# Cells of an mLSTM kernel moved to four ticks for every three units, and the first product of two groups taken as three float32r products

## The chip, the cores and the metric

One NeuronCore of a Trainium2 chip runs the whole kernel. The metric is the device time of the kernel in microseconds. Three runs of the kernel before are shown; their median counts.

## What is computed

An mLSTM cell over 4 batches, 8 heads, 768 steps and 40 channels, and behind it a feed-forward layer on its output, 3072 tokens of 320 channels through 2048 hidden ones. The reference, cut to what matters:

```python
for t in range(S):
    m_new = np.maximum(f_gate[:, :, t] + m, i_gate[:, :, t])
    f_stab = np.exp(f_gate[:, :, t] + m - m_new)
    i_stab = np.exp(i_gate[:, :, t] - m_new)
    C = f_stab * C + i_stab * np.einsum('bhd,bhe->bhde', vt, kt)
    n = f_stab * n + i_stab * kt
    y[:, :, t] = o * np.einsum('bhde,bhe->bhd', C, qt) / np.maximum(np.abs(n . qt), 1.0)
x = y.transpose(0, 2, 1, 3).reshape(B * S, H * D)
h = x @ w_in
out = np.maximum(0.01 * h, h) @ w_out
```

## The kernel before

**Chunks and groups.** The 768 steps are cut into NB = 6 chunks of 128. Cell s = 4c + b is chunk c of batch b, all 8 heads: 24 cells. Group g is the feed-forward layer on the 512 tokens (4 batches x 128 steps) of chunk g. Chunk 0 is worked out ahead of everything. After that the loop at the end of the kernel runs six passes, c = 1 to 6: pass c issues the layer of group c - 1 unit by unit, and in the gaps the cells of chunk c. So the cells of chunks 2 to 5 lie beside groups 1 to 4, and group 5 has none.

**A group's units.** `ff_units` makes 16 units of first product (a pair j of 128-column blocks of w_in, each pair in two units: 5 slots of 64 rows x 2 row halves, L759, then Prelu on ScalarE, L767) and for groups 1 to 5 the 14 units of `fast_units`, a Strassen-like second product in 7 products of two row blocks n, in the order p1, p2, p6, p7, p4, p5, p3 (L835). Sums lie on VectorE and GpSimd: p1 makes s1 and s2 (L853, L858), p2 empties its bank at L862, p6 makes s4 (L870) and adds on GpSimd (L868), p7 adds at L876, p4 at L882, both on GpSimd, p5 empties its bank at L887 into both halves of y on VectorE, p3 at L892. The banks of ph and po come from one pool of four (`psf`, tag mm), the cells' from another of four (`psc`).

**A cell.** `u_parts` multiplies k, q and the state's parts (L614, L619) and puts them with the mask weights w into `qn` (L624, VectorE). `u_mix` takes the tanh of o (ScalarE), multiplies (L695, pT), turns and scales the result on VectorE and GpSimd (L702, L706, L709, L713), carries the state on (L592 on GpSimd, L596 on VectorE) and stores x to DRAM (L716). `ahead(s)` prepares a cell: `prep_kq` turns k and q into kqT (L505, L511, VectorE), the loads of k, q and ea for cell s + 2 are issued (L398, L421), and the state and k are scaled on GpSimd. `feed(s)` loads k, v and w (L356, L359, L413). `prep_mask` adds the mask to w on GpSimd (L450). `gather_x` loads a cell's x back as xT, whose one buffer serves group after group (L730).

**What sets the order.** Instructions of TensorE, VectorE, ScalarE and GpSimd run in the order in which the code issues them (`manual_schedule`). Only SyncE's queue, through which nearly all transfers go, is ordered by the framework. Per group of 30 units i the table below places the cells' nine units (two u_parts, two u_mix, two u_parts, the gates, two u_mix) and the masks; o and the feed follow a u_mix, `ahead` follows it too, but not between i = 16 and 23.

```python
masks = {0: (2, 3), 12: (4, 5)}
pairs = (2, 2, 6, 6, 14, 14, 19, 19, 19)
```

Of the kernel before, what the change touches and what calls it, by code (L numbers as in the profile page):

```python
# [10 lines left out]
U32 = mybir.dt.uint32  # L11
U64 = mybir.dt.uint64
# [6 lines left out]
def kernel(  # L19
# [58 lines left out]
    dr = ctx.enter_context(tc.tile_pool(name="dr", bufs=1, space=bass.MemoryType.DRAM))  # L78

# [39 lines left out]
    kn = consts.tile([P, NL, H, DP], F32, name="kn")  # L119
    qn = consts.tile([P, NL, H, DP], F32, name="qn")  # L120
    S_t = [consts.tile([P, 2, H, DP], F32, name=f"S{n}") for n in range(NL)]
    S_v = [t[:].rearrange("p u h (k d) -> p u h k d", d=QW) for t in S_t]
    rb_t = [consts.tile([P, 3, RW], F32, name=f"rb{n}") for n in range(NR)]
    xb = consts.tile([P, PR * TB, QW], F32, name="xb")
# [147 lines left out]
    def gates(c):  # L272
# [5 lines left out]
        F = wk.tile([n, P], F32, name="F", bufs=1)  # L278
        nc.vector.tensor_tensor_scan(F[:], fc, zeros[:n].to_broadcast([n, P]), 0.0, op0=ALU.add, op1=ALU.add)
        if c > 0:  # L280
            il_t = wk.tile([BH, P], F32, name="il", bufs=1)
            nc.vector.tensor_scalar(il_t[:], il, scalar1=m0[:], scalar2=None, op0=ALU.subtract)
            il = il_t[:]
        m = wk.tile([n, P], F32, name="m", bufs=1)
        nc.vector.tensor_tensor_scan(m[:], fc, il, -1e30 if c == 0 else 0.0, op0=ALU.add, op1=ALU.max)
        a = wk.tile([n, P], F32, name="a", bufs=1)
        nc.vector.tensor_tensor(a[:], F[:], m[:], op=ALU.subtract)
        bu = wk.tile([BH, 3, P], F32, name="bu", bufs=1)
# [117 lines left out]
    def spread(s):  # L406
# [3 lines left out]
        w = wk.tile([P, H, P], F32, name="w", bufs=NL)  # L410
# [4 lines left out]
    def spread_q(s):  # L415
# [3 lines left out]
        d["ea"] = wk.tile([P, H, SL], F32, name="ea", bufs=EAB)  # L419
# [5 lines left out]
    def spread_first(a, s2):  # L425
# [12 lines left out]
        for n in range(2):  # L438
            w = st[s2 + n]["w"] = wk.tile([P, H, P], F32, name="w", bufs=NL)
# [20 lines left out]
    def prep_vu(s):  # L460
# [3 lines left out]
        if s < NS:  # L464
            d["vu"] = wk.tile([P, H, 2, V1], F32, name="vu")
# [34 lines left out]
    def prep_kq(s):  # L500

        d = st[s]
        d["kqT"] = wk.tile([P, 2, PR * P], F32, name="kqT")
# [20 lines left out]
    def u_split(s):  # L524

        d = st[s]
        d["kqT"] = wk.tile([P, 2, PR * P], F32, name="kqT")
# [14 lines left out]
    def u_transpose(s):  # L542
        d = st[s]
        d["kqT"] = wk.tile([P, 2, PR * P], F32, name="kqT")
# [92 lines left out]
    def u_values(s):  # L637
# [4 lines left out]
        d["den"] = wk.tile([P, H], F32, name="den")  # L642
        denominators(d["den"][:], pa[:, :, D])

    def gate(s):

        d = st[s]
        d["x"] = wk.tile([P, Dm], F32, name="x")
# [7 lines left out]
    def u_plain(s):  # L656
# [13 lines left out]
        den = wk.tile([P, H], F32, name="den")  # L670
        denominators(den[:], hN[:, :, 0, DB])
        if b < 2:
            d["x"] = wk.tile([P, Dm], F32, name="x")[:]
# [10 lines left out]
    def u_mix(s):  # L684
# [16 lines left out]
        hb = wk.tile([P, PR * TB, QW], F32, name="hb", bufs=1)  # L701
        nc.vector.transpose(hb[:].rearrange("p (j n) d -> p j n d", n=TB), in_blocks(pT[:]))  # L702
        den = wk.tile([P, PR * TB], F32, name="den")
# [8 lines left out]
        xq = wk.tile([P, PR * P], F32, name="x")  # L712
# [6 lines left out]
    def gather_x(s):  # L719

        c, b = divmod(s, B)
        if ("xT", c) not in st:
            st["xT", c] = wk.tile([P, KC, GT], F32, name="xT", bufs=1)
        xT = st["xT", c]
# [410 lines left out]
```

## Time and profile before

| What | us |
|---|---|
| three runs | 514.08, 512.78, 509.91 |
| their median | 512.78 |
| span of the profiled execution (no time beside it is given) | 508.0 |
| TensorE busy in it | 492.0 |
| VectorE busy | 308.1 |
| ScalarE busy | 171.5 |
| GpSimd busy | 137.7 |

Lines such as L759 are lines of the kernel before. PE is TensorE's matmuls, PEld its weight loads, DVE VectorE, ACT ScalarE, POOL GpSimd, SP SyncE. A name with q behind it (SPq) is that engine's own instruction queue, which issues transfers and waits. A busy TensorE is not one at its peak, since matmuls overlap.

### The profile page before, as it was taken

How to read it: one execution, taken by the hardware profiler on the slowest of the kernel's cores; microseconds unless marked ns; L12 is line 12 of the kernel's file. 1: busy time of each engine (PE TensorE's matmuls, PEld its weight loads, DVE VectorE, ACT ScalarE, POOL GpSimd, SP SyncE). 2: the span in 40 equal slices, each digit the busy share in tenths (PEclk: the TensorE clock that was granted, in tenths of full speed). 3: DMA queues.
4: the chain of work that ended last, by engine and by line, in shares of the span. 5: the costliest groups of instructions: out<-in, count | busy, mean ns of one | idle time of the engine just before them, and what ended most of it. 6: DMA issues, size and time to landing. Idle time of an engine off the chain costs nothing.

```text
span 508.0 us, 12526 instructions
## 1 busy us (share of the span) xinstructions
PE 492.0 (97%) x4981; PEld 366.6 (72%) x4981; DVE 308.1 (61%) x515; ACT 171.5 (34%) x478; POOL 137.7 (27%) x175
## 2 busy tenths in 40 slices
PE   8878999999999999999999999999899999999997
PEld 7766878767655489955589855599755599744797
DVE  4779898899954778635765826764825664101321
ACT  3664864652722510323411323311213411022210
POOL 4243443360402404413104614014612003000020
PEclk9877999999999999999999999999999999999999
DMA  9977687888765551565663566564466212200001
GB/s 116 146 204 154 149 219 185 168 152 175 155 145 87 131 124 46 133 130 144 147 132 92 115 137 170 137 141 97 109 135 177 68 53 62 69 1 1 1 1 52
DMA packets 165290, 59.21 MB, mean 117 GB/s; under 512 B 128816, under 2 KB 156016, under 8 KB 165232
## 3 DMA queue, kind: packets, MB, share of 16 engines
q1 hardware_dynamic: 164848, 58.28, 52.2%
q8 instruction: 39, 0.64, 0.5%
q14 instruction: 19, 0.16, 0.1%
q10 hardware_dynamic: 384, 0.13, 0.1%
HBM read 51.68 MB, written 6.70 MB: 115 GB/s over the span
## 4 chain that ended last, share of the span: by engine, by line
PE 79%; DVE 9%; DMA 3%; ACT 3%; POOL 2%; issue 2%; SPq 2%; ACTq 0%; POOLq 0%; DVEq 0%
PE ph L759 36%; PE po L835 26%; PE po L794 6%; PE pT L695 3%; PE sd L614 3%; SPq L359 1%; PE sd L619 1%; DMA S<-in_v_dram 1%; ACT kqT L540 1%; PE tkq L548 1%; DVE raw L261 1%; DMA rb<-in_q_dram 1%; DMA w<-a_dr 1%; PE pa L641 1%; DVE qn L511 1%
## 5 line engine op out<-in xcount | busy, mean ns | idle before, releaser
L759 PE MATMUL ph<-xT,w_in 64*128 64x512 f32 (+1 forms) x1120 | 216.2, 538 | 2.4 <-DVE y L887 1.4
L759 PEld LDWEIGHTS ph<-xT,w_in 64*128 64x128 f32 x1120 | 108.6, 189 | 95.1 <-issue 86.3
L767 ACT ACTIVATE acts<-ph 128x512 f32<-128x512 f32 (+1 forms) x112 | 53.9, 533 | 179.0 <-PE ph L759 178.9
L835 PEld LDWEIGHTS po<-w_out,acts 128*128 128x128 f32 x640 | 87.3, 190 | 3.8 <-issue 3.8
L835 PE MATMUL po<-w_out,acts 128*128 128x160 f32 x640 | 89.1, 300 | 0.0
L450 POOL TENSOR_TENSOR w<-w,i 128x512 f32<-128x512 f32 x20 | 26.9, 1345 | 117.3 <-DMA w<-a_dr 117.2
L624 DVE TENSOR_TENSOR qn<-w,sd 64x512 f32<-64x512 f32 x40 | 27.4, 684 | 40.2 <-PE sd L619 20.5
L458 ACT ACTIVATE w<-w,gT 128x64 f32<-128x64 f32 (+1 forms) x192 | 50.8, 348 | 2.7 <-POOL w L450 1.7
L592 POOL TENSOR_TENSOR S<-S,f 40x336 f32<-40x336 f32 x36 | 32.0, 889 | 67.3 <-PE pT L695 36.3
L835 PE MATMUL po<-raw,acts 128*128 128x160 f32 x320 | 45.5, 300 | 0.0
L835 PEld LDWEIGHTS po<-raw,acts 128*128 128x128 f32 x320 | 43.9, 190 | 0.3
L794 PE MATMUL po<-w_out,acts 128*128 128x320 f32 x128 | 36.5, 436 | 0.0
L702 DVE STREAM_TRANSPOSE hb<-pT 128x512 f32<-128x512 f32 x16 | 11.5, 717 | 31.0 <-PE pT L695 30.8
L794 PEld LDWEIGHTS po<-w_out,acts 128*128 128x128 f32 x128 | 23.6, 190 | 9.3 <-issue 0.3
L511 DVE TENSOR_TENSOR qn<-kqT,ea 64x512 f32<-64x512 f32 x32 | 28.4, 888 | 1.0
L709 POOL TENSOR_TENSOR xb<-xb,den 128x320 f32<-128x320 f32 x16 | 11.7, 729 | 56.8 <-DVE xb L706 56.6
L596 DVE TENSOR_TENSOR S<-S,sd 40x336 f32<-40x336 f32 x36 | 18.1, 503 | 12.1 <-POOL S L592 11.2
L614 PEld LDWEIGHTS sd<-kqT 40*64 40x64 f32 x640 | 19.9, 135 | 6.1 <-issue 6.1
L822 DVE TENSOR_TENSOR raw<-acts 128x1024 f32<-128x1024 f32 x10 | 11.8, 1222 | 18.3 <-ACT acts L767 18.2
L713 DVE STREAM_TRANSPOSE x<-xb 128x512 f32<-128x512 f32 x16 | 18.2, 1140 | 7.6 <-POOL xb L709 7.6
L835 PE MATMUL po<-raw 128*128 128x160 f32 x160 | 22.5, 299 | 0.0
L835 PEld LDWEIGHTS po<-raw 128*128 128x128 f32 x160 | 22.0, 190 | 0.0
(151 smaller groups left out, 551.8 us busy)
## 6 DMA issues: line engine op xcount, KB each, us to landing
w<-a_dr SPq DMA_DIRECT2D x40, 128.0 KB
rb<-in_k_dram SPq DMA_DIRECT2D x64, 80.0 KB
rb<-in_q_dram SPq DMA_DIRECT2D x64, 80.0 KB
rb<-in_o_gate_dram SPq DMA_DIRECT2D x64, 80.0 KB
ea<-a_dr SPq DMA_DIRECT2D x32, 128.0 KB
kn<-in_k_dram SPq DMA_DIRECT2D x24, 160.0 KB
raw<-in_moe_w_out_dram SPq DMA_DIRECT2D x6, 640.0 KB
S<-in_v_dram SPq DMA_DIRECT2D x80, 40.0 KB
```

The lines of the kernel that those rows point to most:

```text
L450: nc.gpsimd.tensor_tensor(w, w, cm2.unsqueeze(1).to_broadcast([P, H, SL]), op=ALU.add)
L458: yield nc.scalar.activation(w[:, h, :], w[:, h, :], AF.Exp, bias=gT[c][:, 0, bh : bh + 1], scale=1.0)
L511: nc.vector.tensor_tensor(mixed(s)[rows, 1 - r], d["kqT"][rows, 1].rearrange("p (h t) -> p h t", t=SL), d["ea"][rows], op=ALU.mult,)
L592: nc.gpsimd.tensor_tensor(new, old, g, op=ALU.mult)
L596: nc.vector.tensor_tensor(new, new, st[s]["dC", u], op=ALU.add)
L614: nc.tensor.matmul(bank[1 - u][toks, h, :], lhsT=kqT[rows, 0, ts(h, SL)], rhs=kqT[rows, 1, ts(h, SL)], start=True, stop=True,)
L624: nc.vector.tensor_tensor(mixed(s)[toks, u], w[toks], bank[1 - u][toks], op=ALU.mult)
L713: nc.vector.transpose(in_blocks(xq[:]), xb[:].rearrange("p (j n) d -> p j n d", n=TB))
L759: nc.tensor.matmul(ph[r][:, cols], lhsT=w_row(r, slot, j), rhs=xT[DP * r : DP * (r + 1), slot, cols], start=(slot == 0), stop=(slot == KC ...
L767: nc.scalar.activation(acts[:, f, cols], ph[r][:, cols], AF.Prelu, alpha=0.01)
L794: nc.tensor.matmul(po[n][:], lhsT=acts[:, f, ts(n, P)], rhs=w_out[:, f, :], start=(f == 0), stop=(f == NF - 1),)
L835: nc.tensor.matmul(bank[:], lhsT=left[:, f, :], rhs=right[:, f, :], start=f == 0, stop=f == KH - 1)
```

## The change

The cells' tiles move from the pools consts and wk into two pools of their own, cc and cw. The first pass of the loop stays as it was, written out for itself. In the later passes time is counted in ticks, 30 a chunk: unit u (counted from group 1) issues the ticks below (u + 1) * 4 // 3, so that the cells of chunks 2 to 5 (ticks 0 to 109) lie in groups 1 to 3. `masks`, `pairs` and the rule for `ahead` go by the tick, no longer by the group's unit. x is gathered once the first product of the group ahead is issued.

At tick 109 the cells' pools are closed and a pool kp takes their memory. w_in is copied there (raw), and for every half block and every cell of group 4 the low part and a difference are worked out: the top bits by a mask on VectorE, then a subtraction and a multiply-add; for w the subtraction is on GpSimd and a scaled copy on ScalarE. Two to three of these steps follow each unit. Group 4 takes its first two pairs j as before, its other six, and all eight of group 5, as triples: raw x raw and low x low into one bank, dif x dif into another, all in float32r, and ScalarE and VectorE join them to the float32 product before Prelu.

The diff, cut to its core; the other cell tiles change their pool as kn and w do, and the first pass, written out, is left out:

```diff
+F32R = mybir.dt.float32r
+    cells_stack = ctx.enter_context(ExitStack())
+    cc = cells_stack.enter_context(tc.tile_pool(name="cc", bufs=1))
+    cw = cells_stack.enter_context(tc.tile_pool(name="cw", bufs=2))
...
-    kn = consts.tile([P, NL, H, DP], F32, name="kn")
+    kn = cc.tile([P, NL, H, DP], F32, name="kn")
...
-        w = wk.tile([P, H, P], F32, name="w", bufs=NL)
+        w = cw.tile([P, H, P], F32, name="w", bufs=NL)
...
-            st["xT", c] = wk.tile([P, KC, GT], F32, name="xT", bufs=1)
-        xT = st["xT", c]
+            st["xT", c] = wk.tile([P, KC, GT], F32R if c in THREE else F32, name="xT", bufs=1)
+        xT = st["xT", c][:].bitcast(F32)
...
+    EPS = 2.0**-12
+    THREE = (NB - 2, NB - 1)
+    parts = {}
+    def open_parts():
+        cells_stack.close()
+        kp = ctx.enter_context(tc.tile_pool(name="kp", bufs=1))
+        for key in ("raw", "low", "dif"):
+            parts["w", key] = [kp.tile([P, WC], F32R, name=f"w_{key}{n}") for n in range(QN)]
+        for key in ("low", "dif"):
+            parts["x", key] = kp.tile([P, KC, GT], F32R, name=f"x_{key}")
+        parts["tmp"] = [kp.tile([P, KC, P], F32, name=f"tmp{n}") for n in range(2)]
+        parts["tmp_x"] = kp.tile([P, KC, P], F32, name="tmp_x")
+        parts["n"] = 0
+    def tmp_part():
+        parts["n"] += 1
+        return parts["tmp"][parts["n"] % 2]
+    def top_bits(dst, src):
+        nc.vector.tensor_scalar(
+            dst.bitcast(U32), src.bitcast(U32), scalar1=0xFFFFF000, scalar2=None, op0=ALU.bitwise_and,
+        )
+    def fetch_w_part(n):
+        nc.sync.dma_start(parts["w", "raw"][n][:].bitcast(F32), w_in[:, n, :])
+    def split_w_parts(n, half):
+        at = ts(half, WC // 2)
+        src = w_in[:, n, at]
+        held = []
+        def first():
+            t = tmp_part()[:].rearrange("p k t -> p (k t)")
+            held.append(t)
+            top_bits(t, src)
+            nc.gpsimd.tensor_tensor(t, t, src, op=ALU.subtract)
+        def second():
+            t = held[0]
+            nc.vector.scalar_tensor_tensor(
+                parts["w", "dif"][n][:, at], in0=t, scalar=1.0 + 1.0 / EPS, in1=src, op0=ALU.mult, op1=ALU.add,
+            )
+            nc.scalar.activation(parts["w", "low"][n][:, at], t, AF.Copy, scale=1.0 / EPS)
+        return first, second
+    def split_x(s):
+        c, b = divmod(s, B)
+        cols = ts(b, P)
+        src = st["xT", c][:, :, cols].bitcast(F32)
+        t = parts["tmp_x"][:]
+        low = parts["x", "low"][:, :, cols]
+        top_bits(t, src)
+        nc.vector.tensor_tensor(low, t, src, op=ALU.subtract)
+        nc.vector.scalar_tensor_tensor(
+            parts["x", "dif"][:, :, cols], in0=low.bitcast(F32), scalar=1.0 + 1.0 / EPS, in1=src, op0=ALU.mult, op1=ALU.add,
+        )
+    def three_units(g, lead):
+        xs = {"raw": st["xT", g], "low": parts["x", "low"], "dif": parts["x", "dif"]}
+        def rows(j, ph, key, start, stop):
+            n, e = divmod(j, 2)
+            for slot in range(KC):
+                at = (2 * slot + e) * P
+                for r in range(2):
+                    part = slice(DP * r, DP * (r + 1))
+                    nc.tensor.matmul(
+                        ph[r][:], lhsT=parts["w", key][n][part, at : at + P], rhs=xs[key][part, slot, :],
+                        start=start and slot == 0, stop=stop and slot == KC - 1,
+                    )
+        def triple(j):
+            ph, pe = [], []
+            def first():
+                ph.extend(psf.tile([P, GT], F32, name=f"ph{r}", tag="mm") for r in range(2))
+                rows(j, ph, "raw", True, False)
+            def second():
+                rows(j, ph, "low", False, True)
+            def third():
+                pe.extend(psc.tile([P, GT], F32, name=f"pe{r}", tag="c") for r in range(2))
+                rows(j, pe, "dif", True, True)
+                fs = [acts[:, f_of(r, j), :] for r in range(2)]
+                for r in range(2):
+                    nc.scalar.activation(fs[r], pe[r][:], AF.Copy, scale=-EPS)
+                for r in range(2):
+                    nc.vector.scalar_tensor_tensor(
+                        fs[r], in0=ph[r][:], scalar=1.0 + EPS, in1=fs[r], op0=ALU.mult, op1=ALU.add,
+                    )
+                for r in range(2):
+                    nc.scalar.activation(fs[r], fs[r], AF.Prelu, alpha=0.01)
+            return [first, second, third]
+        pairs, seconds = ff_units(g)
+        units = pairs[: 2 * lead] + [u for j in range(lead, NF // 2) for u in triple(j)]
+        for n in range(2):
+            at = 2 * lead + 3 * (KH // 2 + 1 + n - lead) - 1
+            units[at] = lambda n=n, u=units[at]: (u(), mix_early(n))
+        return units, seconds
...
-        xT = st["xT", g]
+        xT = st["xT", g][:].bitcast(F32)
-        return firsts + fast_units(g)
+        return firsts, fast_units(g)
...
-        for c in range(1, NB + 1):
-            if c > 1:
-                ffs = ff_units(c - 1)
...
+        cells = cell_units(1)
...
+        TICKS = 30
+        ENDS = TICKS * (NB - 3) + pairs[-1]
+        units, mixed_steps, after = {}, [], []
+        def before_tick(t):
+            c, i = divmod(t, TICKS)
+            c += 2
+            exps()
+            for n in masks.get(i, ()) if c < NB else ():
+                if c * B + n < NS:
+                    prep_mask(c * B + n)
+        def after_tick(t):
+            c, i = divmod(t, TICKS)
+            c += 2
+            if c + 1 < NB and i == 0:
+                gates(c + 1)
+            if c + 1 < NB and i == 2:
+                gates_exp(c + 1)
+            if i == 0:
+                units[c] = list(zip(pairs, cell_units(c))) if c < NB else []
+            new = []
+            while units[c] and units[c][0][0] <= i:
+                fn, s = units[c].pop(0)[1]
+                fn(s)
+                if fn is u_mix:
+                    mixed_steps.append(s)
+                    after.append(s + 2)
+                    new.append(s)
+            gather()
+            if i < NF or i >= NF + 8:
+                for s in after:
+                    ahead(s)
+                after.clear()
+            for s in new:
+                load_late(s + NR, 2)
+                if s + NL < NS:
+                    feed(s + NL)
+        def gather():
+            while at["past"] and mixed_steps and mixed_steps[0] // B == at["group"] + 1:
+                gather_x(mixed_steps.pop(0))
+        LEAD = 2
+        todo = []
+        def prepare(n):
+            for _ in range(n):
+                if todo:
+                    todo.pop(0)()
+        def split_steps():
+            halves = [(n, half) for n in range(QN) for half in range(2)]
+            steps = [split_w_parts(*h) for h in halves]
+            xs = [lambda b=b: split_x(at["group"] * B + B + b) for b in range(B)]
+            order = [steps[0][0], steps[1][0], steps[0][1], steps[2][0], steps[1][1], steps[3][0], steps[2][1], xs[0], xs[1]]
+            order += [steps[4][0], steps[3][1], xs[2], xs[3]]
+            for m in range(5, len(steps)):
+                order += [steps[m][0], steps[m - 1][1]]
+            return order + [steps[-1][1]]
+        at = {"past": False}
+        t = 0
+        for g in range(1, NB):
+            firsts, seconds = three_units(g, LEAD if g == THREE[0] else 0) if g in THREE else ff_units(g)
+            ffs = firsts + seconds
+            at.update(group=g, past=False)
+            for i in range(len(ffs)):
+                at["past"] = i >= len(firsts) - 1
+                upto = min(ENDS + 1, (TICKS * (g - 1) + i + 1) * 4 // 3)
+                for m in range(t, upto):
+                    before_tick(m)
+                if g == 1 and i == 0:
+                    mixed_weights()
+                for m in range(t, upto):
+                    after_tick(m)
+                gather()
+                if t <= ENDS < upto:
+                    open_parts()
+                    for n in range(QN):
+                        fetch_w_part(n)
+                    todo = split_steps()
+                t = max(t, upto)
+                prepare(3 if i < len(firsts) else 2)
+                if g + 1 < NB and g in THREE and i in range(len(firsts) + 4, len(firsts) + 12, 2):
+                    split_x((g + 1) * B + (i - len(firsts) - 4) // 2)
```

## The prediction

> **What bounds the kernel now.** I read the busy time by group first (the windows view, cut where the chain shows the groups' first products begin), because a mean over the span would mix the start with the steady part.
>
> ```profile
> core 0: us, PE busy (x) PEld busy (x) DVE busy (x) ACT busy (x) POOL busy (x), PEclk, DMA share, GB/s
> 139.40:214.20 74.80, 74.80 (x776) 54.16 (x776) 49.25 (x76) 21.45 (x65) 21.27 (x25) 1.00 0.49 109
> 214.20:289.10 74.90, 74.90 (x776) 54.17 (x776) 46.08 (x81) 21.05 (x64) 24.07 (x26) 1.00 0.56 129
> 289.10:365.20 76.10, 74.76 (x774) 54.05 (x774) 46.42 (x78) 21.14 (x64) 23.56 (x26) 1.00 0.58 130
> 439.80:508.00 68.20, 65.15 (x384) 45.78 (x384) 11.98 (x17) 11.03 (x24) 3.14 (x6) 1.00 0.04 13
> ```
>
> Groups 1 to 4 last 74.8 us each and TensorE fills them, but for 1.3 us in group 3; group 5, which has no cells beside it, takes its two products and a tail. The chain of waits gives the prices on TensorE:
>
> ```profile
> 78.45 6.68 PE ph L759 x60
> 146.45 0.17 PE sd L614
> 148.51 8.78 PE ph L759 x40
> 157.29 2.02 PE pT L695 x64
> 439.79 34.53 PE ph L759 x160
> 474.33 30.64 PE po L835 x224
> ```
>
> A first product is 160 instructions in 34.53 us: 215.8 ns each at 512 columns, 4.32 us for a pair j of column blocks. A group's cells are the rest, 74.8 - 34.5 - 30.7 = 9.6 us: two u_parts take 2.05 us (146.45 to 148.51), two u_mix 2.02.
>
> Then I looked at what has no busy row at all, SyncE's DMA queue (SPq), in its timeline; columns are start, length, line, transfer, count.
>
> ```profile
> 237.15 5.40 SPq L716 DMA_DIRECT2D x_dr<-x  x8
> 242.65 1.80 SPq L398 DMA_DIRECT2D rb<-in_k_dram  x4
> 244.54 1.88 SPq L398 DMA_DIRECT2D rb<-in_q_dram  x4
> 246.53 1.09 SPq L421 DMA_DIRECT2D ea<-a_dr  x2
> ...
> 261.07 1.95 SPq L398 DMA_DIRECT2D rb<-in_o_gate_dram  x4
> 263.07 0.43 SPq L356 DMA_DIRECT2D kn<-in_k_dram  x1
> 263.60 2.69 SPq L359 DMA_DIRECT2D S<-in_v_dram  x4
> 266.33 1.40 SPq L413 DMA_DIRECT2D w<-a_dr  x2
> 267.83 6.02 SPq L730 DMA_DIRECT2D xT<-x_dr  x8
> ```
>
> The queue issues without a gap. Where nothing holds it back, two cells cost it 3.7 us of x_dr (315.38 to 319.05), 10.5 of k, q and ea (300.49 to 311.1), 4.1 of o, 9.6 of feeds (kn, S and w) and 5.3 of gathers: 33.2 us, plus some 1 us of out and a_dr. Groups of 74.8 us carry two such pairs, so SP has 37.4 us for each: 90% full. Its order is nearly that in which the code emits the transfers, so w comes last of a pair's loads. The waits and the chain show who feels that:
>
> ```profile
> POOL w L450 <- DMA w<-a_dr: 117.2, 13, 22.9
> ```
>
> ```profile
> 344.26 3.33 DMA w<-a_dr
> ...
> 347.74 1.24 POOL w L450
> 349.06 0.76 POOL S L592
> 349.90 0.74 POOL xb L709
> 350.66 1.12 DVE x L713
> ...
> 364.97 0.24 DVE y L887
> ```
>
> GpSimd sits in prep_mask until w lands, up to 22.9 us, with all its later work behind it; then VectorE, and in group 3 at last TensorE's first ph, waiting for the bank that L887 empties: the 1.3 us. So TensorE bounds the kernel, with the SP queue next and almost no margin.
>
> **The change, part by part**, against the profiled span of 508.0 us. The page gives no time of that execution beside its span; the median shown, 512.78, is 4.8 above it, and I carry that difference.
>
> *Products.* A pair j in float32 is 5 slots x 2 row halves x 2 instructions; the halves run side by side, so each slot costs 863 ns, four streams of 512 columns at 215.8. The float32r form has no row. I take one stream for each of 3 x 5 slots: 15 x 215.8 = 3.24 us, 1.08 less a pair j. Fourteen pairs (6 in group 4, 8 in group 5): **-15.1**. The weight load must hide under one stream; nearest is group 0's half-width product, 60 instructions in 6.68 us, 111 ns each, or one pair of loads every 223 ns, which would still give -13.8. Upper end: two streams a slot, 6.47 us, +2.16 a pair j, +30.2. I take the first, since the change sends three products where the instruction it replaces streams four times. A rule of the Trainium skill speaks against it: "TensorE: Matmul & The Clock Gate", Part 3 (Packing small matmuls), lets a weight load overlap matmuls in flight only where the row group differs, though its Part 2 also knows a background buffer. By Part 3 loads would stand in line with their own half's stream. The trace disagrees for float32: there the 111 ns leave no room for the 189 ns of a load.
>
> The epilogue of a pair j adds four ScalarE ops of 0.59 (L767's row at 512 columns), 2.4 us, and two VectorE ops of about 0.7 (L624's 684 ns); both lie below 3.24, with two sets of banks to run ahead. ph is held longer; nothing.
>
> *Cells at 4/3.* The same TensorE work moves from group 4 into groups 1 to 3: 0, and the 1.3 us stall there goes (**-1.3**) if nothing takes its place. Something does. Groups 1 to 3 become 65.2 + 4/3 x 9.6 = 78.0 us long with 2.67 pairs of cells, 29.3 us a pair; SP needs about 33. Over the seven intervals between eight pairs that is some 26 us short, which TensorE must wait out somewhere. I place it by going through the ticks (tick t runs at the first unit u with (u+1)*4//3 > t, units counted from group 1):
>
> (a) Start of group 2. u_mix(12, 13) falls at unit 27, after the second p5, with ahead(14, 15) in the same tick. VectorE's row for two u_mix and two aheads is 232.0 to 246.9, 14.9 us; the two L892 that empty p3's banks stand behind it. TensorE has 2.0 + 2 x 2.2 + 4.3 = 10.7 us until the second pair's ph wants those banks. **+5** (ends 0 and 10: the first if VectorE has slack I don't see, the second if k and q for cell 15 are as late as SP's ledger allows).
>
> (b) Middle of group 2: u_parts(16, 17) at unit 47 wants kqT, behind a prep_mask that waits for w(17). **+3** (0 to 7).
>
> (c) End of group 2, the dearest. u_mix(16, 17) is at unit 50 and emits the loads of w(20) and w(21). prep_mask(20, 21), tick 72, is at unit 54, just ahead of p4, so both L882 stand behind it on GpSimd. L887 of p5 overwrites what L882 reads and waits; behind L887 on VectorE stand the L624 of u_parts(18, 19); and u_mix(18, 19) at unit 59 needs them. From u_mix to the second mask's end before took 40.2 us (232.0 to 272.2) and 42.1 (306.9 to 349.0); L882, L887 and L624 add 3. TensorE gets from unit 50 to 59 in 2.0 + 9 x 2.2 + 2.2 + 0.7 = 24.7. Wait: 18.5 to 20.4 if SP is as little behind as then; my count of SP's items has it about 11 us later, with group 3's gather in front, so 31 at the most. If SP issued w first, as it did at 150.6 in group 1 where it was idle, 0. I take **+22**, near the rows. (a) to (c) make 30, the ledger's 26 by another way.
>
> *Opening the parts* at unit 82. VectorE gets 9 us of u_mix(22, 23), then steps of w (mask 0.6, L259; multiply-add 1.05, L257) and x (0.6 + 0.9 + 1.05 = 2.55 a cell): 14 steps, some 18 us, ahead of the last L892, and possibly a wait for x_dr to leave the memory (some 4). That is 29 to 34 us, against 2.0 + 7 x 2.2 + 4.3 = 21.8 until group 4's second pair j wants p3's bank: **+7** (0 to 12). The later steps lie beside TensorE's work. The four copies of raw weights (655 KB each) queue on SP after x_dr; raw of block 1 is wanted 26 us after the opening. At the 117 GB/s that section 3 of the profile gives, an estimate for two is 11.2 us: hidden, 5 at worst.
>
> Sum: 508.0 - 15.1 - 1.3 + 5 + 3 + 22 + 7 = 528.6; with 4.8, **533.4 us**.
>
> **The rivals.**
> - *The queue keeps up* (the other side). SP sends w(20) and w(21) before x_dr, k and q, so (b) and (c) vanish and VectorE alone costs 3 at (a) and 4 at the opening: 508.0 - 16.4 + 7 + 4.8 = 503.4. For it: group 1 shows kn and w issued ahead of x_dr. Against: from 214 on the order is as emitted, and a fuller queue has no idle place for that. It decides when w(21) lands less than 24.7 - 3 - 1.3 = 20 us after unit 50.
> - *Half the wait*: (c) comes to some 8 us, and the opening to 3: about 515.
> - *The products gain nothing*: loads in line with their streams, 15 x (216 + 189) = 6.1 us, +1.8 a pair j, +25 instead of -15: 573. For it: only that no float32r row exists. By that rule of the Trainium skill this is the outcome; the trace of float32 disagrees.
>
> **How the numbers follow.** Forecast 0.70 (own range 517 to 550); queue keeps up 0.14; half the wait 0.09; products 0.07. The range of **504 to 556** leaves out half of the second and the last, and the forecast's tail above 550 by little. A measurement of this kernel can tell about 1% from no change: faster 0.14, same 0.08 (most of half the wait), slower 0.78.
>
> **What would show it.** A first product of group 5 of about 26 us instead of 34.5 (products right). An SP queue without gaps from 180 to 330; TensorE idle before the L695 of the third chunk's second pair, with VectorE in L887, GpSimd in L450 and w at the end of that chain (c); idle at the second ph of group 2 behind L892 (a), and of group 4 (opening). Wrong it is if GpSimd's waits at L450 get no nearer to TensorE, or if a triple takes over 4.3 us.

## The result, and the profile after

The kernel after takes 559.99 us (median of four runs, 558.55 to 562.66), the one before 511.35 on the same chip: a ratio of 1.0955 (95% interval 1.0898 to 1.1012), slower by 48.6 us. The forecast was 533.4, with an upper end of 556: the sign is right, the loss is more than twice the one expected.

Lines from L356 to L730 moved by four, those from L759 on by 113: the mask add L450 is now L454, w's load L413 is L417, the first product L759 is L872, the second L835 is L948, L882 is L995, L887 is L1000, L892 is L1005.

The windows view of the changed kernel, cut at the groups' first products, answers to the first fence of the prediction (there groups 1 to 3 are 74.8 to 76.1 us long, and TensorE's one gap is of 1.3 us):

```profile
core 0: us, PE busy (x) PEld busy (x) DVE busy (x) ACT busy (x) POOL busy (x), PEclk, DMA share, GB/s
137.98:218.23 80.25, 79.53 (x969) 58.08 (x968) 59.59 (x106) 26.19 (x83) 28.08 (x30) 1.00 0.55 120
218.23:345.93 127.70, 87.46 (x975) 64.68 (x974) 59.04 (x106) 22.99 (x70) 35.51 (x34) 0.85 0.60 134
496.40:558.00 61.60, 58.41 (x464) 52.73 (x464) 22.10 (x33) 20.75 (x40) 3.13 (x6) 1.00 0.04 14
```

Three rows show most of the story; group 4 with the opening, 9.4 us of idle time, is not among them. Group 1 is 80.3 us long, near the 78.0 forecast for a group with 4/3 of the cells. Group 2 is 127.7. Group 5 is 61.6 instead of 68.2, so the new products pay. The clock of 0.85 in group 2 had no place in the prediction.

Who waits in group 2 is told by the waits view of the changed kernel (total, times, longest):

```profile
POOL w L454 <- DMA w<-a_dr: 89.6, 7, 29.9
ACT rb L498 <- DMA rb<-in_o_gate_dram: 48.1, 5, 25.7
DVE hn L1000 <- POOL hn L995: 35.6, 1, 35.6
PE tg L332 <- DVE S L600: 31.6, 1, 31.6
```

Before, GpSimd's wait for w was 22.9 us at the longest and TensorE felt 1.3 us of it; now three engines stand behind one load, one after the other. The chain of waits shows the order, from SP's issue to TensorE (start, length, what):

```profile
331.72 0.62 SPq L417
...
332.39 3.61 DMA w<-a_dr
...
337.35 0.53 POOL hn L995
...
338.14 0.32 DVE y L1000
...
340.89 0.69 DVE qn L628
...
342.25 3.68 PE pT L699 x64
```

And SP's timeline shows why w(21) goes out only at 331.72, though the two u_mix that its cells waited for ran from 283.8 on:

```profile
293.02 11.92 SPq L734 DMA_DIRECT2D xT<-x_dr  x16
...
306.14 3.05 SPq L720 DMA_DIRECT2D x_dr<-x  x8
...
331.72 1.26 SPq L417 DMA_DIRECT2D w<-a_dr  x2
```

From 204 to 333 the queue waits some 13 us in all, 5.8 of them for an x to store that is itself late behind a w. From 293 to 333 its one wait in the waits view is 0.6 us: it only issues, and a whole group's gather (11.9 us) stands in front.

The second half of the change works as meant. Two lines of the chain in group 4, one triple (raw and low in 20 instructions, dif in 10):

```profile
448.47 2.32 PE ph L809 x20
450.79 1.13 PE pe L809 x10
```

3.45 us, against 4.32 for a pair j in float32.

### The profile page after: what moved, and what is told of

It reads as the page before. It is cut to its first block, busy times and chain, and to the rows that moved or that the text cites. A ratio compares the mean times of both kernels' runs of the same rounds, so it can differ in the third digit from the quotient of the medians.

```text
span 558.0 us, 12963 instructions
## 1 busy us (share of the span) xinstructions
PE 495.6 (89%) x5121; PEld 389.6 (70%) x5121; DVE 359.4 (64%) x583; ACT 194.4 (35%) x514; POOL 161.9 (29%) x183
## 4 chain that ended last, share of the span: by engine, by line
PE 63%; DVE 11%; SPq 10%; DMA 5%; POOL 4%; issue 4%; ACT 2%; DVEq 0%; POOLq 0%; ACTq 0%
PE po L948 20%; PE ph L872 18%; PE ph L809 6%; PE po L907 5%; DMA w<-a_dr 3%; SPq L402 3%; PE pe L809 3%; PE pT L699 3%; PE sd L618 2%; SPq L363 2%; SPq L734 2%; PE pa L645 2%; POOL tmp L775 1%; DVE x L717 1%; PE warm L326 1%
## 5 line engine op out<-in xcount | busy, mean ns | idle before, releaser
L872 PE MATMUL ph<-xT,w_in 64*128 64x512 f32 (+1 forms) x840 | 162.5, 532 | 12.1 <-ACT acts L880 6.1
L872 PEld LDWEIGHTS ph<-xT,w_in 64*128 64x128 f32 x840 | 84.2, 195 | 79.5 <-issue 56.8
L948 PE MATMUL po<-w_out,acts 128*128 128x160 f32 x640 | 92.1, 304 | 1.8 <-ACT hn L994 1.8
L948 PEld LDWEIGHTS po<-w_out,acts 128*128 128x128 f32 x640 | 89.1, 193 | 5.3 <-issue 2.2
L880 ACT ACTIVATE acts<-ph 128x512 f32<-128x512 f32 (+1 forms) x84 | 38.6, 513 | 108.2 <-PE ph L872 108.1
L454 POOL TENSOR_TENSOR w<-w,i 128x512 f32<-128x512 f32 x20 | 34.4, 1722 | 97.2 <-DMA w<-a_dr 89.6
L596 POOL TENSOR_TENSOR S<-S,f 40x336 f32<-40x336 f32 x36 | 33.2, 922 | 59.2 <-PE hN L669 29.5
L948 PE MATMUL po<-raw,acts 128*128 128x160 f32 x320 | 45.7, 300 | 0.7 <-DVE acts L971 0.7
L948 PEld LDWEIGHTS po<-raw,acts 128*128 128x128 f32 x320 | 44.0, 190 | 1.1 <-issue 0.9
L1000 DVE TENSOR_TENSOR hn<-hn,po 128x160 f32<-128x160 f32 x10 | 3.2, 317 | 57.8 <-POOL hn L995 35.6
L981 POOL TENSOR_TENSOR y<-y,raw 128x160 f32<-128x160 f32 x10 | 9.1, 907 | 98.1 <-ACT y L980 98.1
L831 DVE SCALAR_TENSOR_TENSOR acts<-ph,acts 128x512 f32<-128x512 f32 x28 | 18.0, 686 | 28.1 <-ACT acts L829 28.1
L628 DVE TENSOR_TENSOR qn<-w,sd 64x512 f32<-64x512 f32 x40 | 27.3, 683 | 10.8 <-PE sd L623 5.8
L332 PE MATMUL tg<-ident,bu 32*128 32x32 f32 x13 | 2.1, 253 | 32.3 <-DVE S L600 31.6
L498 ACT ACTIVATE rb<-rb 128x320 f32<-128x320 f32 x20 | 8.8, 469 | 49.1 <-DMA rb<-in_o_gate_dram 48.1
L332 PEld LDWEIGHTS tg<-ident,bu 32*128 32x128 f32 x13 | 1.5, 162 | 34.7 <-issue 34.5
```

The lines of the kernel that those rows point to most:

```text
L454: nc.gpsimd.tensor_tensor(w, w, cm2.unsqueeze(1).to_broadcast([P, H, SL]), op=ALU.add)
L596: nc.gpsimd.tensor_tensor(new, old, g, op=ALU.mult)
L628: nc.vector.tensor_tensor(mixed(s)[toks, u], w[toks], bank[1 - u][toks], op=ALU.mult)
L831: nc.vector.scalar_tensor_tensor(fs[r], in0=ph[r][:], scalar=1.0 + EPS, in1=fs[r], op0=ALU.mult, op1=ALU.add,)
L872: nc.tensor.matmul(ph[r][:, cols], lhsT=w_row(r, slot, j), rhs=xT[DP * r : DP * (r + 1), slot, cols], start=(slot == 0), stop=(slot == KC ...
L880: nc.scalar.activation(acts[:, f, cols], ph[r][:, cols], AF.Prelu, alpha=0.01)
```

## The experiments

Theory 1, that of the prediction: at the new pace SP's issue time for two cells (some 33 us) is more than the 29.3 us there are, the queue falls behind, and TensorE waits at the one place where a chain runs from w's load to it. Rival 2: that place alone is at fault (masks issued too early, behind them L995), and SP would keep up. Rival 3: landing times and the freeing of buffers, not issue time. Each edit is against the changed kernel if nothing else is said.

**The pace alone.**

```diff
-    THREE = (NB - 2, NB - 1)
+    THREE = ()
...
-                if t <= ENDS < upto:
+                if THREE and t <= ENDS < upto:
```

> The changed kernel without the float32r products: cells at 4/3 of the pace, all groups with the float32 product of the kernel before, no opening of the parts. Theory 1 (the pace costs): the waits in group 2 stay; 558 less 9.4 us of idle time at the opening and some 5 us of low clock there, plus 12.1 us that the triples gain: span 552 to 560. Rival (the new products and the preparation of their parts cost most of the loss): span 510 to 520.

553.6 us, ratio 1.085 (1.076 to 1.096), with the same stall of 31.1 us. The pace carries the loss. Products and opening together seem to cost some 6 us more than they bring, though the intervals of the two kernels overlap.

**The masks later.**

```diff
-        masks = {0: (2, 3), 12: (4, 5)}
+        masks = {0: (2, 3), 20: (4, 5)}
```

> The changed kernel with one number moved: the masks of the next chunk's first two cells at tick 20 instead of 12, so that prep_mask(20, 21) no longer stands on GpSimd in front of p4's two L882 (L995 in the changed kernel). Theory 1 (the SP queue is short of time; the mask is only where that comes out): w, o, k and q of a pair still land as late, so the 31.6 us in which TensorE stood before the third chunk's last u_mix shrink, but the tanh of o(18) and o(19), which landed at about 324 and 331, then holds ScalarE and its Prelu: 10 to 20 us are lost elsewhere, span 536 to 548. Theory 2 (the place of the mask on GpSimd alone is the cause): all of the 31.6 us and some 4 us of low clock behind it go, span about 522.

536.0 us, 1.051 (1.042 to 1.060). The wait at L332 is gone, GpSimd's at L454 is 6.8 us at the longest, and TensorE stops a little further on:

```profile
328.27 15.46 PE L872 MATMUL ph<-xT,w_in 64*128 64x512 f32 x60 [11.29 <-ACT acts L880]
```

The number in brackets is idle time before the line. Here ScalarE's Prelu L880 stands behind a tanh (L498) that waits for a late o block, another load of the same queue. A late queue finds its next reader, so rival 2's 522 is out. But the profiled span of 534.9 us also lies a little below the 536 to 548 that theory 1 gave, so the place of the mask counts for somewhat more than I had it.

**The feed ahead of the gather.** o and the feed of the next cell are emitted before `gather()` and `ahead`.

```diff
+            for s in new:
+                load_late(s + NR, 2)
+                if s + NL < NS:
+                    feed(s + NL)
             gather()
...
-            for s in new:
-                load_late(s + NR, 2)
-                if s + NL < NS:
-                    feed(s + NL)
```

> The changed kernel with o and the feed (k, v, w) of a pair issued before the gathers and before ahead's k, q and ea; nothing else moved, and SP has as much to do. Theory 1: w and o come some 10 us earlier after each u_mix: the 31.6 us before the third chunk's last u_mix become 18 to 24, ScalarE's wait for o(14) with TensorE's 4.2 us goes, span 534 to 550; since SP is as full as before, not all of it goes. Rival (the total of SP's time is no matter, only the order in which it is spent): all waits in groups 1 to 3 go, span 512 to 520.

544.3 us, 1.066 (1.063 to 1.070); the stall is 23.2 us instead of 31.6 and the one behind L498 gone. The order of the queue is worth some 15 us, not the whole, as theory 1 had it.

**Eight more issues a cell, in the kernel before.** The opposite dose: eight small transfers (4 KB, to a scratch array that nobody reads) on SP behind each u_mix of chunks 2 to 5.

```diff
                     if fn is u_mix:
                         waiting.append(s)
+                        for n in range(8):
+                            nc.sync.dma_start(more_dr[8 * s + n], ident[:16, :64])
```

> The kernel before, at its old pace, with 8 more transfers of 4 KB each on SP's queue after every u_mix of chunks 2 to 5 (to a scratch array that nobody reads): 16 a pair of cells, some 0.45 to 0.5 us of issue each, 0.5 MB in all. Theory 1 (SP's issue time binds): a pair needs 33 + 8 = 41 us of a queue that has 37.4, so TensorE, idle for 1.4 us before, loses 15 to 35 us, in groups 2 to 4, behind GpSimd's wait at prep_mask. Rival (bytes or DMA engines bind, not the issuing): 0.5 MB of 59 changes nothing, span 508 to 511.

536.4 us, 1.051 (1.048 to 1.054), +26.5, inside the 15 to 35 of theory 1; the rival had none. Eight of them take 3.56 us of SP, 16 times 57 us. The prediction's ledger gave SP 37.4 - 33.2 = 4.2 us to spare a pair, 33.6 over eight pairs; 57.0 - 33.6 = 23.4 should come through. That 26.5 did is near in part by luck: TensorE's idle stretches there are 17.4 us (1.4 before), 7.5 of them for an x that SP gathered late, and low clock takes some 7.7 more. SP's longest hold of GpSimd grows from 22.9 to 31.9 us.

**Fewer issues in the changed kernel.** First without the o blocks of cells 12 on (`i == 2` in place of `i in (0, 2)`), then without k's as well. These cells work with what older cells left in the buffer, so the two kernels are experiments only:

```diff
-        elif s < NS:
+        elif s < NS and not (i in (0, 2) and s >= 3 * B):
             load_blocks(s, i)
```

> The changed kernel without the loads of the output gate's blocks for cells 12 on (these cells use the gate of older cells that is still in the buffer; all other work stays). It takes 4 issues of some 0.5 us a cell off SP, 2 us a cell, 8 cells before the masks of cells 20 and 21: theory of SP's issue time: the stall of 31.6 us falls by about 16 to some 12 to 18 us, the 4.2 us behind prep_o go, and with the clock 535 to 542 us. Rival, that the stall is set by what the masks' a rows wait for and not by the queue's length: the stall stays over 25 us and the time at 550 to 556 us.

> The changed kernel without the loads of the output gate's and of k's blocks for cells 12 on (these cells use what older cells left in the buffer; all other work stays): twice the relief of the run without the o blocks, 8 issues or some 4 us a cell off SP. Theory of SP's issue time, one microsecond of the time for each microsecond of SP's queue until the stall is used up: the stall before the first look at the gates of group 4 falls from 22.7 us (o blocks left out) to 5 to 10 us, and the time from 544.5 to 525 to 531 us. Rival, a remainder that SP's issues do not set (landing of the a rows, the freeing of buffers): the stall stays at 17 us or more and the time at 538 us or more.

Without o 544.5 us, 1.066 (1.060 to 1.072); without o and k 517.7 us, 1.015 (1.011 to 1.020). TensorE at the end of group 2, first without o, then without o and k:

```profile
323.60 0.39 PE L332 MATMUL tg<-ident,bu 32*128 32x32 f32 x2 [22.69 <-DVE S L600]
```

```profile
300.39 0.30 PE L332 MATMUL tg<-ident,bu 32*128 32x32 f32 x2
```

The first dose (eight cells at 2 us each by then) takes some 15 us off the time; the stall itself falls by only 8.9, less than I expected, because the 4.2 us stall behind L498 goes too and TensorE comes to this place 7.9 us earlier. Together that is 16.8, near the 16 of SP's time that the dose frees. The second removes the stall altogether and beats my 525 to 531; rival 3 would have kept 17 us. These doses take transfers away as well as issues; the dose in the kernel before added issues with hardly any bytes (0.5 MB of 59), and the two together speak for the issues.

What is left without o and k adds up: from the span of 508.0, less 1.4 for the old stall and 12.1 for the triples, plus 15.0 of idle stretches and 6.3 of low clock, it comes to 515.8, which is the span.

**Moving issues to ScalarE's queue.** Three tries: the feeds of cells 12 on; with masks at 20 and feed first, the gathers, one cell a unit and eight ticks behind its u_mix; with the same two, the k blocks. No run has masks at 20 and feed first with everything on SP, so the last two can't be told apart from those edits.

```diff
-        nc.sync.dma_start(d["k"][:, :, :D], k[b, :, rows, :].rearrange("h p d -> p h d"))
+        queue = nc.scalar if c > 2 else nc.sync
+        queue.dma_start(d["k"][:, :, :D], k[b, :, rows, :].rearrange("h p d -> p h d"))
```

> The changed kernel with the feeds of cells 12 to 23 (k, v and w: 7 issues a cell) on ScalarE's queue instead of SP's. Theory 1 (SP's issue time binds): SP's load falls from 33 to some 24 us for a pair that takes TensorE 29.3, GpSimd's waits at prep_mask fall below 10 us each, TensorE's idle time in groups 1 to 3 from 41 us to under 8; with 494.6 us of work at full clock and 9 to 14 us for the opening of the parts, span 504 to 518. Rival (the transfers themselves or the DMA engines are too slow at this pace, and the queue only shows it): w lands as late as before and the span stays within 5 us of 558.

```diff
-                nc.sync.dma_start(xT[DP * r : DP * (r + 1), at : at + n, ts(b, P)], src[:, k0 : k0 + 2 * n - 1 : 2, :])
+                nc.scalar.dma_start(xT[DP * r : DP * (r + 1), at : at + n, ts(b, P)], src[:, k0 : k0 + 2 * n - 1 : 2, :])
```

> As the run before, with the mask at tick 20 as well, and with the gathers (4 issues a cell) on ScalarE's queue, one cell a unit, from 8 ticks after the cell's u_mix on, when its x has landed. SP then needs some 28 us a pair, ScalarE 1.8 to 2.6 us more in a unit of a second product, where it has only copies of 0.3 us to do. Theory 1: SP is below TensorE's 29.3 us a pair, idle time of TensorE in groups 1 to 3 falls below 10 us, and with 494.6 us of work and 14 us of idle time and low clock at the opening the span is 508 to 520. Rival (a queue on ScalarE stalls whatever waits behind it, as in the run with the feeds there): 530 to 550.

```diff
-                nc.sync.dma_start(
+                (nc.scalar if i == 0 and s >= 3 * B else nc.sync).dma_start(
```

> The changed kernel with the masks at tick 20, the feed of the next cell issued before the gather, and the k blocks of cells 12 on issued by ScalarE (their buffer's readers have all been issued before, so ScalarE should not be held by them; 4 issues a cell, some 4 us of SP's 33 a pair). Theory of SP's issue time: SP keeps up with the pace of 29.3 us a pair, the stall of 31.6 us and that of ScalarE behind the late o blocks go, the opening stays: 512 to 522 us with 10 to 16 us idle. Rival, that landing times and the freeing of buffers set the order and not the issue time (ScalarE's queue takes the place of SP's): 530 to 545 us.

561.8 us (1.101, 1.095 to 1.108), 539.5 (1.060, 1.054 to 1.065) and 570.2 (1.118, 1.111 to 1.125): all three slower than theory 1 gave. The first is where its rival put it (span 558.5, within 5 us of 558), but not for the rival's reason: GpSimd's longest wait for w falls from 29.9 to 8.4 us, and the stall of 31.6 goes. TensorE loses the time elsewhere, with four waits of 4.6 to 11.5 us for ScalarE. The second is in the 530 to 550 of its rival; the third is above both forecasts. ScalarE with the k blocks, in its timeline and in the source view of the line (ns of one issue: shortest, median, longest):

```profile
278.86 12.82 ACTq L402 DMA_DIRECT2D rb<-in_k_dram  x8
291.73 1.09 ACT L880 ACTIVATE acts<-ph 128x512 f32<-128x512 f32 x2 [17.53 <-DMA rb<-in_k_dram]
```

```profile
L402 ACTq DMA_DIRECT2D rb<-in_k_dram x48: 317/352/501, 161.4 to 366.7; - x48
```

ScalarE's Prelu waits behind these issues, and TensorE stood 10.7 us there for its bank. The issues themselves are short, 0.35 us each against 0.45 on SP; the 12.8 us are mostly pauses of 2.7, 3.4 and 3.2 us between them. Each pause ended within 0.1 us of the landing of one of SP's transfers, on whose semaphore the next issue waited: w at 281.85, S at 286.21, w at 290.79. In the run with the gathers SP waited in turn: 8.4 us at once for a gather of ScalarE's to land, before it could store x. So the two queues were not independent here, and these runs are no clean test of theory 1: it is landing times that hold them, as rival 3 has it, once two queues issue. The Trainium skill, "DMA: Bandwidth & Descriptors", section "Issuing engines are not separate DMA queues", has it that a second issuing engine saves only the sequencer's time, "which is usually small relative to the DMA itself". Here that time was what bound the kernel, by the two doses above; a second engine took it off SP, and lost it again in these waits.

**The new products by themselves.** At the old pace (`// 3` and `* 4` taken out), only group 5 in three products, from pair j = 2 on.

```diff
-    THREE = (NB - 2, NB - 1)
+    THREE = (NB - 1,)
...
-                upto = min(ENDS + 1, (TICKS * (g - 1) + i + 1) * 4 // 3)
+                upto = min(ENDS + 1, TICKS * (g - 1) + i + 1)
```

> The other part alone: cells at the old pace of one tick a unit, so that they end in group 4, and the float32r products in group 5 only, in its last six pairs j; the steps of w lie in group 4's second product, those of x in group 5's first two units. Theory 1: 508.0 less 1.3 less 6 x 0.87 = 501.5, plus up to 6 us where VectorE is late: span 501 to 508. Rival (preparing the parts costs more than the products give, wherever it is put): span 511 to 518.

w's steps come first there, x's last, with six empty steps between. 518.7 us, 1.016 (1.008 to 1.023), where its rival put it: six triples bring 5.2 us, but 11.9 us of idle time, 10.4 of them at the opening, and the clock take more. I took most of it to stand behind GpSimd's subtraction, so that went to VectorE, first here, then in the changed kernel with masks at 20, feed first and k on ScalarE:

```diff
-            nc.gpsimd.tensor_tensor(t, t, src, op=ALU.subtract)
+            nc.vector.tensor_tensor(t, t, src, op=ALU.subtract)
```

> Against the run with the old pace and three products in group 5 alone (518.7 us, idle stretches of TensorE of 11.9 us together, most of them behind GpSimd's subtraction of w): the same kernel with that subtraction on VectorE (16 instructions, about 1 us each). Theory: GpSimd's queue and the longer VectorE steps beside it make those stalls; they go, what is left is the wait of the first step for its columns of x (some 3 us) and the products' gain of 10 pairs x 0.87 us: 505 to 510 us, idle 2 to 6 us, VectorE's steps back at 0.5 and 0.8 us. Rival: the splitting as a whole comes too late for the products, whatever engine does it, and VectorE with 16 us more work holds the Prelu's and y's banks as long as GpSimd did: 514 to 519 us.

> The run with the masks at tick 20, the feed first and the k blocks on ScalarE, and the subtraction of w on VectorE besides. Theory: the opening's stalls (9.4 us in the changed kernel, with a clock of 0.80 to 0.81 around them) are GpSimd's subtraction and fall to 2 to 5 us: 5 to 8 us below the run without it, at 505 to 516 us, so about the kernel before. Rival: the opening is bound by VectorE's and ScalarE's queues: the same as the run without it, within 2 us.

515.6 us, 1.011 (1.006 to 1.015), and 568.8 (1.114, 1.108 to 1.120) against 570.2: both times are where the rivals had them, so the subtraction was not most of it. Idle time fell to 8.1 us in the first (6.4 of them at the opening; its profile is of the slowest of six executions, 520.6 us), and at the opening of the second from some 10.8 to 8.8. The steps did get shorter (groups view; L775 is the subtraction, L779 a multiply-add and L758 the mask on VectorE). With it on GpSimd:

```profile
L779 DVE SCALAR_TENSOR_TENSOR w_dif<-tmp,w_in 128x640 fp32r<-128x640 f32 x8 | 11.5, 1441 | 1.4 <-POOL tmp L775 1.4
L758 DVE TENSOR_SCALAR tmp<-w_in 128x640 uint32<-128x640 uint32 x8 | 8.7, 1101 | 3.6 <-DMA x_dr<-x 2.9
```

and on VectorE:

```profile
L779 DVE SCALAR_TENSOR_TENSOR w_dif<-tmp,w_in 128x640 fp32r<-128x640 f32 x8 | 6.8, 857 | 0.0
L758 DVE TENSOR_SCALAR tmp<-w_in 128x640 uint32<-128x640 uint32 x8 | 4.1, 510 | 3.5 <-DMA x_dr<-x 2.9
```

What is left is a burst: once x_dr has landed and the memory is handed over, VectorE runs some 20 us of splitting without a pause, and y's additions (L1000), which free TensorE's banks, stand behind. So the steps were spread out, and the empty ones left out:

```diff
-        LEAD = 2
+        LEAD = 4
...
-                prepare(3 if i < len(firsts) else 2)
+                prepare(2 if i < len(firsts) else 1)
```

> The run with the old pace, three products in group 5 alone and the subtraction on VectorE, with the splitting spread out: one step a unit in group 4's second product (two in group 5's first), no empty steps, and the first four pairs of group 5 as plain float32 (six in three products). Theory: the 8.1 us of idle stretches were the burst of splitting steps ahead of VectorE's additions; they fall to 1 to 3 us, the products gain 6 x 0.87 = 5.2 us: 504 to 509 us, faster than the kernel before by 0.3 to 1.3 per cent. Rival: VectorE has no room for the steps whatever their spacing, or the columns of x come too late: 511 to 516 us.

> As the run with four plain pairs ahead, with three (seven in three products, 6.1 us gained). Theory: 503 to 508 us, within 1 us of the run with four. Rival: the split columns of x are not ready for the first triple, which waits 1 to 3 us and brings the clock down: 1 to 5 us above the run with four.

> The fastest version so far (505.3 us) with the subtraction of w back on GpSimd. If spreading the steps alone took the stalls away: 504 to 508 us, with VectorE's steps longer beside GpSimd's but no idle stretch on TensorE behind them. If GpSimd's subtraction was the cause: stalls of 4 to 8 us behind ScalarE's copies and 509 to 515 us.

A group has eight pairs j, so there are six triples in the first two of these kernels and four or five in the last three; where their expectations name a number, ten, six and seven, it is too high. With four plain pairs ahead 505.3 us, 0.991 (0.989 to 0.994): **0.9% below the kernel before**, with the whole interval below 1 but by less than 2%, and with no idle stretch at the opening. That it lies in the 504 to 509 forecast is in part luck, since six triples were counted there: the four bring 3.5 of the 5.4 us, and the rest is not explained. With three 510.7 us, 0.998 (0.994 to 1.002): the first triple waits 2.9 us for x's low part, as its rival had it, and the time is 5.4 us above the run with four, a little over the rival's 1 to 5. With four, and the subtraction back on GpSimd, 509.9 us, 0.999 (0.996 to 1.003): no gain without both edits, and the spreading (with the two more plain pairs ahead) is the larger, since without the other it takes the idle time at the opening from 10.4 to 2.0 us. These 2.0 us do not account for all of the 4.6 between the last and the best; the clock is 1.00 over the groups in both.

Last, the kernel without the late o and k blocks, with this opening:

> The changed kernel without the o and k blocks' loads of cells 12 on (517.7 us; these cells use what older cells left in the buffer), with the splitting spread as in the fastest version: one step a unit, two in a first product, four plain pairs ahead, the subtraction on VectorE. Theory: the opening's 10 us of idle fall to 1 to 3 us, 12 triples instead of 14 give 10.4 us, the stall of 3.9 us in group 2 stays: 501 to 508 us. Rival: at the new pace other work stands where the steps go (the late cells' work), the opening stays: 513 to 518 us.

507.0 us, 0.994 (0.992 to 0.996), 10.7 below the same without it. So the most that the change reached in these runs, with SP relieved of loads that it needs, is some 3 us under the kernel before.

**Is the triple set by its weight loads?** Only 64 of the 128 columns of w are loaded and multiplied.

```diff
-                        ph[r][:], lhsT=parts["w", key][n][part, at : at + P], rhs=xs[key][part, slot, :],
+                        ph[r][:DP], lhsT=parts["w", key][n][part, at : at + DP], rhs=xs[key][part, slot, :],
```

> The changed kernel with the triples on 64 of each block's 128 hidden columns: the other 64 of these blocks are left out. Streams stay 512 columns long, only the loads of weights get half as wide. The triples' instructions came every 115 ns, 230 us a thousand pairs of row halves, against 215.8 for the float32 stream. Theory A (the load of weights sets this pace, at 183 ns a load): a pair of row halves falls to 216 to 220 ns and a triple from 3.45 to about 3.25 us. Theory B (float32r streams at 230 ns by itself, or row halves don't quite overlap): 3.45 us stays.

Loads fall from 184 to 137 ns; the triple stays, at 3.47 us (562.6 us in one run). So the width of the loads does not set the 115 ns an instruction. Whether the stream itself takes that long or the two row halves do not quite overlap, theory B's two ways, no run tells apart.

## Why the prediction was right in sign and wrong in size

In us, against the span of 508.0:

| Step | Forecast | In the trace |
|---|---|---|
| products, 14 triples | -15.1 | -12.1 |
| stall of 1.3 in group 3 | -1.3 | -1.3 |
| (a) second ph of group 2 | +5 | +0.7 |
| (b) u_parts(16, 17) | +3 | +2.5 |
| (c) end of group 2 | +22 | +32.2 |
| ScalarE behind o, 254.9 | none | +4.2 |
| other gaps of cells | none | +1.4 |
| opening | +7 | +9.4 |
| clock | none | +10.1 |
| not placed | none | +2.9 |
| sum | 20.6 | 50.0 |

The 29.4 us between the two sums are 10.2 of (c), 10.1 of clock, 4.2 of ScalarE, 3.0 of products, 2.4 of the opening, 1.4 and 2.9 of smaller rows, less 4.8 that (a) and (b) were too high.

- **(c), mis-sized.** Place, chain and cause are those of the prediction, link by link; the idle time shows at the gates' product L332, issued just ahead of that u_mix. TensorE had 25.0 us from u_mix (283.8) to the stall (308.8), forecast 24.7; L995, L1000 and L628 added 3.1, forecast 3. What failed is "I take +22, near the rows": from u_mix to the second mask's end it took 53.6 us, not the rows' 40.2 to 42.1. My own count of SP's items had said about 11 us more, 31 in all, and I put it at the end of the range. The rows belonged to a queue that still had slack; the count had the change in it. With 31 the sum would still have been 542.4, so the clock had to be in it as well.
- **The clock, left out.** It was a cost of its own. The windows view of the changed kernel (stretch, its length, TensorE's busy time, granted clock, DMA share, GB/s):

```profile
250.70:254.90 4.20, 0.03 (x2) 1.00 0.75 160
254.90:266.00 11.10, 11.07 (x41) 0.85 0.41 102
308.80:340.40 31.60, 0.02 (x1) 0.57 0.62 136
340.40:350.00 9.60, 8.99 (x86) 0.63 0.50 136
```

  After the pause of 4.2 us the granted clock is 0.85 over 11.1 us of full work, after 31.6 us it is 0.63 over 9.6. Counted in steps of 4 us (busy time times what is missing from 1.00) it makes 10.1 us over the groups: 1.4 behind the first of these, 3.2 behind the second, 3.8 at the opening, and 1.7 behind the two pauses of 1.0 and 1.5 us of (b), with only small products between them. The Trainium skill, "TensorE: Matmul & The Clock Gate", Part 1, says that an idle window of about 3.4 us halves the clock; the trace agrees, with 0.50 in all slices from 314 to 342. A forecast with 22 us of stalls in it had to carry a price for the work behind them.
- **ScalarE behind o, not seen.** The prediction followed SP's lateness to GpSimd only. The o blocks go out just ahead of w, and ScalarE waits for them with Prelu behind.
- **(a), too high.** At the second pair ph was given banks that the first pair's Prelu had just emptied, not p3's: L1005 ran only at 228.5, the product at 223.4. I had assumed that banks are taken in turn. It is not settled by rule either: in the kernel without o and k the same product did wait for L1005, 3.9 us, so the mechanism of (a) is real and its +5 nearly right where the bank is p3's.
- **Products.** The mechanism holds (three float32r streams, with the loads hidden under them, in place of four of float32); the rival with loads in line, 6.1 us a pair j, does not. The size was off: 230 ns a pair of row halves instead of 215.8 makes -12.1 of -15.1.
- **Opening.** Right in place and near in size. At the old pace the runs showed two causes that I had lumped: VectorE's burst, the larger, and its steps' length beside GpSimd. At the new pace the second alone gave nothing clear; both together took the idle time at the opening from 10.4 to 2.1 us.
- **The rivals.** "The queue keeps up" put 503.4. Even without the late o and k loads the kernel stands at 517.7, since (a), the opening and the clock behind them remain; with the opening mended too, 507.0.

What stays open: 2.9 us of the table, why a pair of float32r row halves takes 230 ns, and what moving issues to ScalarE would give if the two queues did not wait on each other's semaphores.

## What to carry to other kernels

A queue that is nine tenths full is a resource like an engine: count its time per unit of work at the new pace. Where that count and a row from a kernel with slack differed, the count was right here (31 against 22; measured 32). Price each stall with the clock behind it (here some 10 us on 50 of idle time). Background work that is moved in front of a bank's reader should be issued one step a unit: the same steps in a burst cost 6 us of TensorE's time here; spread out, with four plain pairs ahead instead of two, none. Before an issue is moved to another engine's queue, look what that queue will wait for: work of the engine stands behind it.

## What the runs showed of the hardware

- A float32r matmul of 64 rows and 512 columns takes 115 ns in a run that alternates between two row halves (30 in 3.45 us), 230 a pair, whether 64 or 128 columns of weights are loaded.
- The clock also fell without a long pause: from 276 to 278 it was 0.50, behind 3.8 us in which TensorE was busy for 1.3 and no pause was longer than 1.5.
- VectorE's steps lengthen beside GpSimd's: 510 to 1101 ns for a mask on 128x640 that reads one tensor, 857 to 1441 for a multiply-add that reads two, while GpSimd subtracts (2068). Within the run with GpSimd the four masks that lay 1.3 us beside a subtraction took 1.63 to 1.65 us, the four that lay at most 0.1 beside one 0.49 to 0.63. The Trainium skill, "Trainium Architecture — The Big Picture", section "What this means for kernel authors", names a port pair that the two share, as an exclusive lock; the numbers agree with sharing, and cannot show the lock.
